# Moving two splits, a maximum and some sums out of the first step of the last stage of a fused kernel

## The chip, the cores and the metric

The kernel runs on one core of a Trainium2 chip. The metric is the device time of one execution, in microseconds (us). Three timed executions of the kernel before gave 990.42, 991.65 and 994.59 us; the median is 991.65 us. All engines (TensorE, here PE, with its weight loads as PEld; VectorE, DVE; ScalarE, ACT; GpSimd, POOL; SyncE, SP, which issues most of the DMAs) run their own instruction lists in program order and wait for one another by semaphores.

## The reference

Three layers in a row, each on the result of the one before:

```python
scores = scale * q @ k.T                       # 4 batches x 8 heads, 576 x 576, head 64
scores = where(scores >= max(scores) - tau, scores, -1e9)
x = softmax(scores) @ v                        # -> 2304 tokens x 512
x2 = ((x @ w1) * (x @ w2)) @ w3 @ w_out        # d_ff 1024
h = x2 @ w_in                                  # d_ff 2048
g = where(h > 0, h, exp(min(h, 0)) - 1)        # ELU
out = g @ w_out2
```

q, k, v and the output are float32, the weights of the last two layers float64.

## The kernel before

The attention and the products x@w1, x@w2 come first; their order is planned by a table, and the change does not touch them. They leave g = (x@w1)(x@w2) in DRAM, and M = w3·w_out in SBUF. What follows is written out by hand: the order of the code is the order on each engine.

**The x stage** makes x2 = g·M. It goes over six blocks of 384 tokens (`TB`), in the order `JS`; a block has four tiles, and tile n = 4·block + e (n = 0 to 23) is 24 matmuls (L1405) into one of four PSUM buffers. Precision is kept by splitting numbers into a high and a low part: g of the next block is loaded by SP into the eight buffers `th`, ACT writes the high parts into `sl` (L326) and DVE the low ones (L327). These eight ACT and eight DVE instructions, called the splits of x→x+1, are issued behind the last tile of each block (n = 3, 7, 11, 15, 19), and the matmuls of the next block read `sl`. ACT copies each finished tile out of PSUM (L1443, L1446), and squares it for a size (L1223, sums in `xm`).

The list `slot[n]` holds other work that is hung behind tile n. For each of four quarters q of w_in (`win_jobs`) it converts two chunks from float64 words to float32 (`conv`: ACT L337, DVE L347, L351, L354), takes their sizes as sums of squares (`size(0)` on ACT, `size(1)` on DVE, L370 and L372, into the columns `wm`), forms four sums s1 to s4 on GpSimd (`both`, L1291), and, for q = 0 and 1, scales and splits the seven parts into `WI` (`directs`: ACT L1313, DVE L1316, the latter called the lows of WI). For q = 2 and 3 the parts are stored in DRAM and split later. The scale needs the size over all partitions: at n = 4, 8, 12 and 16 a matmul with ones on PE (L1227) adds up two columns of `wm`, and DVE reads its result (L1230).

x2's seven sums for the last stage (`BSRC`) are split into `so` / `bs[k]`: high on ACT (`high_b`, L1207), low on DVE (`low_b`, L1211). Three are split in slots, two (k = 3, 4) around the last tile n = 23, and k = 5, 6 in the first step of the last stage.

The chunks of w_out2 (`wo_steps`) are converted, measured and split in `jobs`. A scale for g needs the largest size `wo_two` of any chunk, over all partitions: `everywhere` stores a column of 128 values into DRAM (`mx_dr`, L1006), loads it back as 128 rows of 128 (`mxb`, L1010), and DVE takes the maximum (L1013). Before, a first maximum over four of the eight chunks goes through this at n = 0, 3 and 5, and a second one over all eight at steps 2 and 3 of the last stage.

**The h stage** (the last) has 24 steps s, 8 for each of three pairs of blocks p. A step is seven products (L1555, six matmuls each, two PSUM buffers in turn); product 0 is read by ACT (L1596) and the others by DVE (L1581), which builds four sums `th`; each goes through the ELU (DVE L1481 minimum, ACT L1482 exponential, DVE L1485, ACT L1487 and DVE L1492 for high and low of `gg`). Between the products stand the output matmuls of the step before (L1505, five at a time), none in step 0. GpSimd and ACT split the stored parts of w_in in the same steps (`split_u`: L1388, L1391, L1394, on loads `wr`).

Of the kernel before, what the change touches and what calls it, by code (L numbers as in the profile page):

```python
# [19 lines left out]
P = 128  # L20
# [12 lines left out]
TB = 384  # L33
# [5 lines left out]
ROOM = 2.0 ** -16  # L39
LEAST_X, LEAST = 2.0 ** -45, 2.0 ** -30  # L40
# [229 lines left out]
def attention_moe_moe2(  # L270
# [916 lines left out]
    bs = [slp2.tile([P, 2, 2, TB], F16, name=f"so{i}") for i in range(3)] + [None] * 4  # L1187
# [83 lines left out]
    def win_jobs(q):  # L1271
# [203 lines left out]
    def elu_low(c):  # L1475

        x, name, dst = c["x"], c["name"], c["dst"]

        def one():
            t = c["t"] = tmp("et", f"et{name}", 2)  # L1480
            V.tensor_scalar(t, x, 0.0, None, op0=ALU.min)  # L1481
            A.activation(t, t, AF.Exp)  # L1482

        def two():
            V.scalar_tensor_tensor(x, c["t"], -1.0, x, op0=ALU.add, op1=ALU.max)  # L1485
            h = hop.tile([P, 2, TB], F16, tag="gg", name=f"gg{name}", bufs=8)
            A.activation(h[:, 0, :], x, AF.Copy, scale=c["by"])  # L1487
            dst["h"] = h

        def three():  # L1490
            h = dst["h"]
            V.scalar_tensor_tensor(h[:, 1, :], x, c["by"], h[:, 0, :], op0=ALU.mult, op1=ALU.subtract)  # L1492

        return one, two, three

    def o_mms(p, f, half, dst, first, last):

        j = JS[2 * p + half]
        stop = last or (p == 0 and f == NH // 2 - 1 + (half == 0) * NH)
        again = p == 0 and f % NH >= NH // 2  # L1500
# [41 lines left out]
    for s, (p, f) in enumerate(steps):  # L1542
# [76 lines left out]
        run_jobs(int(s < 3))  # L1619
# [15 lines left out]
        run_jobs(int(s < 3))  # L1635
        if s == 2:
# [4 lines left out]
        if s == 3:  # L1641
# [16 lines left out]
        if s == NH // 2:  # L1658
# [57 lines left out]
```

## Time and profile before

| | |
|---|---|
| timed, three executions | 990.42 / 991.65 / 994.59 us |
| profiled execution | 992.74 us, its span 991.0 us |
| mean granted TensorE clock | 0.988 of full |
| PE busy | 943.4 us, 95% of the span |
| DVE busy | 757.2 us, 76% |
| ACT busy | 572.3 us, 58% |
| POOL busy | 409.2 us, 41% |

A span is the time from the first to the last instruction that the profiler saw; the execution's time is 1.74 us longer. The x stage begins at 509.47 us, the h stage at 621.08 us and ends with the span. In a row of a timeline the first number is the start, the second the time to the end of the group, and the bracket the idle time of the engine before it with what ended it. In a row of a window each engine's busy time stands with its number of instructions, then the granted clock (1.00 is 2.4 GHz, 0.50 is 1.2 GHz), the share of the DMA engines, and GB/s.

### The profile page before, as it was taken

Reading aid. Unit: us, or ns where it says so; the run is one execution under the profiler, and the core shown is the slowest. Engines: PE = TensorE matmul, PEld = TensorE weight load, DVE = VectorE, ACT = ScalarE, POOL = GpSimd, SP = SyncE. Lnnn points to the kernel's source line nnn. Section 1 sums busy time; section 2 is a strip of 40 time slices with the busy share of each in tenths; the row PEclk is TensorE's granted clock in tenths of the full one; section 3 lists DMA queues with packets and bytes.
Section 4 is the critical chain, followed back from the end, with each engine's and each line's share of the span. In section 5 each row is a group of like instructions: output and inputs, shape, how many; then the busy total and the mean of one; then the engine's idle time right before and its main releaser. Section 6 shows DMA issues by size and latency. Waiting matters only on the chain.

```text
span 991.0 us, 17082 instructions
## 1 busy us (share of the span) xinstructions
PE 943.4 (95%) x6086; PEld 692.9 (70%) x6086; DVE 757.2 (76%) x1445; ACT 572.3 (58%) x1003; POOL 409.2 (41%) x553
## 2 busy tenths in 40 slices
PE   7889999989989999999999899699999999999998
PEld 4456788878988988998789899355555555555554
DVE  7889876888777787486668995778878676875664
ACT  5777776888567676255556748654445323542333
POOL 3468775878789897253423312465300000000000
PEclk9999999999999999999999999799999999999999
DMA  8447655565988878775757587232002000010001
GB/s 270 153 131 167 149 166 159 142 177 152 218 166 207 178 170 158 212 260 199 258 147 228 183 270 262 73 107 40 6 1 103 25 1 1 1 64 1 1 1 64
DMA packets 158866, 130.58 MB, mean 132 GB/s; under 512 B 117340, under 2 KB 145468, under 8 KB 154172
## 3 DMA queue, kind: packets, MB, share of 16 engines
q1 hardware_dynamic: 154668, 99.82, 38.0%
q10 hardware_dynamic: 4112, 29.66, 9.2%
q8 instruction: 48, 0.79, 0.3%
q14 instruction: 38, 0.31, 0.1%
HBM read 80.68 MB, written 21.05 MB: 103 GB/s over the span
## 4 chain that ended last, share of the span: by engine, by line
PE 42%; DVE 4%; ACT 3%; issue 1%; DMA 1%; SPq 0%; DVEq 0%; ACTq 0%
PE o L1505 19%; PE h L1555 16%; PE x L1405 6%; DVE sl L327 1%; PE m L1087 1%; DVE w_win L354 0%; ACT WI L1313 0%; DVE WI L1316 0%; DVE w_wo L354 0%; ACT u_win L337 0%; ACT u_win L370 0%; DVE w_w L354 0%; DMA th<-g_dr 0%; DVE th L1581 0%; DVE M L1097 0%
## 5 line engine op out<-in xcount | busy, mean ns | idle before, releaser
L697 PE MATMUL ab<-x,W 128*128 128x256 f32 (+1 forms) x1536 | 223.8, 298 | 5.5 <-DVE g L712 4.4
L697 PEld LDWEIGHTS ab<-x,W 128*128 128x128 f32 x1536 | 207.5, 188 | 14.6 <-issue 6.0
L1505 PE MATMUL o<-WO,gg 128*128 128x512 f16 x864 | 213.8, 380 | 0.0
L1555 PE MATMUL h<-so,WI 128*128 128x384 f16 x1008 | 194.9, 331 | 4.0 <-DVE th L1581 3.4
L1581 DVE SCALAR_TENSOR_TENSOR th<-h,back,th 128x384 f32<-128x384 f32 x168 | 100.8, 613 | 80.8 <-PE h L1555 80.0
L1555 PEld LDWEIGHTS <-WI 128*128 128x128 f16 x1008 | 99.6, 99 | 89.8 <-issue 8.4
L1505 PEld LDWEIGHTS <-gg 128*128 128x128 f16 x864 | 84.9, 98 | 85.6 <-issue 1.3
L537 DVE SCALAR_TENSOR_TENSOR e<-s,st,e 128x576 f32<-128x576 f32 x144 | 115.2, 808 | 24.4 <-ACT e L531 22.0
L548 POOL TENSOR_TENSOR hl<-e,hl 128x512 f16<-128x512 f32 x94 | 110.3, 1173 | 23.7 <-ACT hl L544 20.1
L513 DVE TENSOR_REDUCE st<-s 128x1 f32<-128x576 f32 x144 | 106.0, 749 | 16.0 <-PE s L503 10.0
L1482 ACT ACTIVATE et<-et 128x384 f32<-128x384 f32 x96 | 49.1, 511 | 110.5 <-DVE et L1481 110.5
L1405 PE MATMUL x<-sl,M 128*128 128x384 f32 x576 | 106.8, 345 | 4.8 <-DVE sl L327 3.9
L1405 PEld LDWEIGHTS x<-sl,M 128*128 128x128 f32 x576 | 103.6, 195 | 6.6 <-DVE sl L327 5.5
L531 ACT ACTIVATE e<-s,st 128x576 f32<-128x576 f32 x108 | 78.4, 737 | 25.4 <-POOL st L521 16.5
L1487 ACT ACTIVATE gg<-th,c_late 128x384 f16<-128x384 f32 x80 | 49.2, 615 | 74.0 <-DVE th L1485 73.8
L503 PE MATMUL s<-qk 128*128 128x288 f32 x480 | 82.6, 304 | 4.9 <-DVE e L537 4.0
L544 ACT ACTIVATE hl<-e 128x576 f16<-128x576 f32 x94 | 63.1, 681 | 23.8 <-DMA pt<-hl 14.4
L503 PEld LDWEIGHTS s<-qk 128*128 128x128 f32 x480 | 67.6, 188 | 13.2 <-issue 7.2
L1485 DVE SCALAR_TENSOR_TENSOR th<-et,th 128x384 f32<-128x384 f32 x96 | 54.5, 567 | 6.1 <-ACT et L1482 5.7
L1492 DVE SCALAR_TENSOR_TENSOR gg<-th,c_late,gg 128x384 f16<-128x384 f32 x80 | 49.1, 614 | 0.2 <-ACT gg L1487 0.2
L1087 PE MATMUL m<-WO,w 128*128 128x512 f32 x192 | 44.9, 392 | 2.5 <-DVE M L1097 1.9
L491 PE MATMUL s<-qkp 128*64 128x288 f32 x288 | 40.7, 415 | 6.7 <-ACT pt L589 3.4
(156 smaller groups left out, 1369.9 us busy)
## 6 DMA issues: line engine op xcount, KB each, us to landing
rqk<-in_qk SPq DMA_DIRECT2D x24, 576.0 KB
raw_wo<-in_wo ACTq DMA_DIRECT2D x12, 1024.0 KB
th<-g_dr SPq DMA_DIRECT2D x48, 192.0 KB
raw_w<-in_w SPq DMA_DIRECT2D x8, 1024.0 KB
raw_w<-in_w3t ACTq DMA_DIRECT2D x8, 1024.0 KB
raw_win<-in_win ACTq DMA_DIRECT2D x8, 1024.0 KB
vr<-in_v SPq DMA_DIRECT2D x16, 320.0 KB
g_dr<-g SPq DMA_DIRECT2D x16, 320.0 KB
```

The costliest lines, as they stand in the source:

```text
L503: T.matmul(s[:, n, :HS], q, k[:, c:c + HS], start=(x == 0), stop=(x == len(ops) - 1))
L513: V.tensor_reduce(st[i][:, 0:1], sc[i][:, :, :HS], axis=AX.XY, op=ALU.max if plain else ALU.min, negate=plain)
L531: A.activation(et[i], sc[i][:, :, :HS], AF.Exp, bias=st[i][:, k:k + 1], scale=esc if plain else -1.0)
L537: V.scalar_tensor_tensor(et[i], sc[i][:, :, :HS], st[i][:, 1:2], et[i], op0=ALU.is_ge if p < NPL else ALU.is_le, op1=ALU.mult, accum_out=s ...
L544: A.activation(hl[i][:, :S], et[i].rearrange("p a b -> p (a b)"), AF.Copy)
L548: G.tensor_tensor(t[:, S + 64:], e[:, :512], t[:, :512], op=ALU.subtract)
L697: T.matmul(o[:, :w], wf[:, m, wx, kt, :], x[:, xx, :], start=(kt == 0 and k == 0), stop=(kt == NK - 1 and k == 2),)
L1087: T.matmul(o, w[:, wx, jt * P:(jt + 1) * P], WO1[jt // 2][:, ox, (jt % 2) * 512:(jt % 2) * 512 + 512], start=(k == 0), stop=(k == 23),)
L1405: T.matmul(o[:, :TB], M[:, f, mx, e * P:(e + 1) * P], gh[j, f][:, gx, :], start=(k == 0), stop=(k == 23),)
L1505: T.matmul(po[j, t], dst["h"][:, gx, t * P:(t + 1) * P], WO[f // 2 % 4][:, f // 8, f % 2, wx, :], start=(first and k == 0), stop=(stop and ...
L1555: T.matmul(o[:, :TB], w[:, wx, kt, :], bs[k][:, kt, xx, :], start=(i == 0), stop=(i == 5),)
L1581: V.scalar_tensor_tensor(x, a, bk, b, op0=ALU.mult, op1=ALU.add)
```

## The change

Seven edits, all in the x and h stages; the order of PE's instructions stays as it is. Line numbers of the new kernel are one or two higher here, from the new constant `LATE` on.

1. Five of the `so` buffers are own tiles and two lie in `sl` (three and four before). k = 3 and 4 are split behind n = 20 to 23 in slots, no longer around the last tile.
2. `size(1)` of each quarter moves from beside `conv(1)` to behind the next splits of g (q = 0: from n = 1 to n = 3; q = 1: from 4 to 5; q = 2: from 9 to 11; q = 3: from 13 to 15).
3. GpSimd's four sums of each quarter begin with a copy of one column out of the last `sl`, so they wait for the last split.
4. The first maximum is taken over six chunks, at n = 22, loaded back at n = 23 and read in step 0 behind product 0. The scales of w for pair 0 move from n = 21 to n = 20, and the five small DVE instructions that follow from the maximum (`h_scale`) go behind its reading.
5. With only two late chunks (`LATE` = 6) the rescaling moves from step 4 to 6, the second maximum from step 2 to 4, its reading from 3 to 5, and the last two `h_scale` from step 5 to 7.
6. The jobs of w_out2 run in steps 1 to 3 (0 to 2 before), and `split_u` begins in step 1.
7. In step 0 the ELU's minimum on DVE is replaced by a Relu of −x on ACT.

```diff
-    bs = [slp2.tile(...) for i in range(3)] + [None] * 4
+    bs = [slp2.tile(...) for i in range(5)] + [None] * 2
 ...
         def both():
+            G.tensor_copy(shift, f32(slots[3][:, 1, 1, :1]))
             quarters()
 ...
-        def second():
-            size(0)
-            conv(1)
-            size(1)
-        t0 = ((0, 1, 3), (3, 4, 7), (8, 9, 11), (12, 13, 15))[q]
+        t0 = ((0, 1, 3, 3), (3, 4, 5, 7), (8, 9, 11, 11), (12, 13, 15, 15))[q]
         slot[t0[0]].append(call(conv, 0))
-        slot[t0[1]].append(second)
-        slot[t0[2]].append(both)
+        slot[t0[1]] += [call(size, 0), call(conv, 1)]
+        slot[t0[2]].append(call(size, 1))
+        slot[t0[3]].append(both)
 ...
-    for k, n in enumerate((16, 17, 19)):
+    for k, n in enumerate((16, 17, 19, 20, 22)):
         slot[n].append(call(high_b, k, 0))
-        slot[(17, 19, 20)[k]].insert(0, call(low_b, k, 0))
+        slot[(17, 19, 20, 21, 23)[k]].insert(0, call(low_b, k, 0))
 ...
+    slot[23].append(lambda: behind.pop(0)())
 ...
-            if n == 0:
+            if n == 20:
+                V.tensor_reduce(w_two[:, 4:5], w_two[:, :4], axis=AX.X, op=ALU.max)
+                back_scale((0,))
+            if n == 22:
                 V.tensor_reduce(
-                    shift, cols("wo_two", 8)...[:, :, :2], axis=AX.XY, op=ALU.max
+                    shift, cols("wo_two", 8)...[:, :, :3], axis=AX.XY, op=ALU.max
                 )
                 seen_o = everywhere(shift)
-            if n == 3:
+            if n == 23:
                 seen_o[0]()
-            if n == 5:
-                seen_o[1](o_two[:, 0:1])
-            if n == 21:
-                V.tensor_reduce(w_two[:, 4:5], w_two[:, :4], axis=AX.X, op=ALU.max)
-                back_scale((0,))
-                h_scale((0,), o_two[:, 0:1], c_by)
 ...
-            V.tensor_scalar(t, x, 0.0, None, op0=ALU.min)
-            A.activation(t, t, AF.Exp)
+            if c["first"]:
+                A.activation(t, x, AF.Relu, scale=-1.0)
+                A.activation(t, t, AF.Exp, scale=-1.0)
+            else:
+                V.tensor_scalar(t, x, 0.0, None, op0=ALU.min)
+                A.activation(t, t, AF.Exp)
 ...
-            while ns[0] < min(max(5 * s + k + 1 - (k > 2) - (k > 5), ...
+            while ns[0] < min(max(5 * s - 5 + k + 1 - (k > 2) - (k > 5), ...
 ...
+        if s == 0:
+            seen_o[1](o_two[:, 0:1])
+            h_scale((0,), o_two[:, 0:1], c_by)
 ...
-        run_jobs(int(s < 3))
+        run_jobs(int(0 < s < 4))
 ...
-        if s in (3, 5):
-            h_scale((0,) if s == 3 else (1, 2), o_two[:, 1:2], c_late)
+        if s in (5, 7):
+            h_scale((0,) if s == 5 else (1, 2), o_two[:, 1:2], c_late)
         after(5)
-        if s == NH // 2:
+        if s == LATE:
             rescale(0)
```

On DVE around the splits of x = 2→3 (behind n = 11) the kernel before has, with `w_win_7179` the second chunk of quarter 2, `sl` and `th` the buffers of the splits (the first and the last of eight are shown), and `WI_7168` quarter 1's parts:

```order
L354 SCALAR_TENSOR_TENSOR w_win_7179<-u_win_7177,w_win_7179 128x1024
L372 SCALAR_TENSOR_TENSOR u_win_7177,wm<-w_win_7179 128x1024
L327 TENSOR_TENSOR sl_6377<-th_6381,sl_6377 128x384
...
L327 TENSOR_TENSOR sl_6380<-th_6388,sl_6380 128x384
L1316 SCALAR_TENSOR_TENSOR WI_7168<-s_1_7092,w_to,WI_7168 128x2x256
L1316 SCALAR_TENSOR_TENSOR WI_7168<-w_win_6918,w_to,WI_7168 128x2x256 x2
L1316 SCALAR_TENSOR_TENSOR WI_7168<-w_win_6955,w_to,WI_7168 128x2x256
L1230 TENSOR_REDUCE xg<-x_1_3_7215 128x1
```

and the new kernel, at the same place:

```order
L355 SCALAR_TENSOR_TENSOR w_win_7177<-u_win_7175,w_win_7177 128x1024
L328 TENSOR_TENSOR sl_6377<-th_6381,sl_6377 128x384
...
L328 TENSOR_TENSOR sl_6380<-th_6388,sl_6380 128x384
L1318 SCALAR_TENSOR_TENSOR WI_7166<-s_1_7090,w_to,WI_7166 128x2x256
L1318 SCALAR_TENSOR_TENSOR WI_7166<-w_win_6916,w_to,WI_7166 128x2x256 x2
L1318 SCALAR_TENSOR_TENSOR WI_7166<-w_win_6953,w_to,WI_7166 128x2x256
L373 SCALAR_TENSOR_TENSOR u_win_7175,wm<-w_win_7177 128x1024
L1231 TENSOR_REDUCE xg<-x_1_3_7212 128x1
```

The size that writes a column of `wm` stood ahead of the eight splits and stands behind them and behind four lows of `WI`. PE reads that column with its ones in front of tile 13, in both kernels alike:

```order
L1405 MATMUL x_4_0_7284<-sl_6380,M 128x384 x6
L1227 MATMUL x_4_0_7284<-wm,ones 128x2
L1405 MATMUL x_4_1_7327<-sl_6377,M 128x384 x6
```

On DVE at the start of step 0, the kernel before has the two lows `so` of k = 3 and 4, a piece of a w_out2 conversion, and the first sum of step 0 (L1581, of `h_0_1`):

```order
L1042 RECIPROCAL wo_to<-wo_two 128x1
L1211 SCALAR_TENSOR_TENSOR so_7772<-bq,x_to,so_7772 128x2x384
L1211 SCALAR_TENSOR_TENSOR so_7774<-tq_6728,x_to,so_7774 128x2x384
L347 TENSOR_SCALAR w_wo_7821<-raw_wo_7508 128x1024
L1581 SCALAR_TENSOR_TENSOR th_6382<-h_0_1_7827,back,th_6381 128x384
```

and the new kernel, from the size of the last early chunk to the same sum:

```order
L1043 RECIPROCAL wo_to<-wo_two 128x1
L1429 TENSOR_REDUCE shift<-wo_two 128x1
L1212 SCALAR_TENSOR_TENSOR so_6728<-tq_6730,x_to,so_6728 128x2x384
L1014 TENSOR_REDUCE o_two<-mxb_7741 128x1
L1259 TENSOR_SCALAR out_by<-x_two,w_two 128x1
L1260 TENSOR_SCALAR out_by<-out_by,o_two 128x1
L1261 TENSOR_SCALAR up<-out_by 128x1
L1262 RECIPROCAL up<-up 128x1
L1263 TENSOR_SCALAR c_by<-wo_two,up 128x8
L1575 SCALAR_TENSOR_TENSOR th_6382<-h_0_1_7826,back,th_6381 128x384
```

Between the maximum of a partition (`shift`) and its reading back (`mxb`) there is now one instruction on DVE, and the reading stands ahead of the first sum. SP issues the two transfers around its stores of x2's last tiles:

```order
L1440 DMA x_dr<-x2s_1_7704 128x384
L1007 DMA mx_dr_7739<-shift 128x1
L1440 DMA x_dr<-x2s_2_7742 128x384
L1011 DMA mxb_7741<-mx_dr_7739 128x128
L1440 DMA x_dr<-x2s_3_7775 128x384
L1373 DMA wr_7794<-wi_dr 128x256
```

Before, these two stood a whole block apart among the loads of g, at n = 0 and n = 3.

## Rows read from the trace of the kernel before

**Rows 1.** The page's first part: busy time, share of the span, instructions of each engine.

```profile
PE 943.4 (95%) x6086; PEld 692.9 (70%) x6086; DVE 757.2 (76%) x1445; ACT 572.3 (58%) x1003; POOL 409.2 (41%) x553
```

**Rows 2.** Windows: two stalled blocks, a clean one, steps 0, 1, 3, pair 1's first.

```profile
526.34:546.88 20.54, 19.02 (x99) 18.15 (x98) 16.72 (x26) 12.49 (x29) 6.48 (x5) 0.92 0.64 200
563.80:587.63 23.83, 20.55 (x102) 19.72 (x101) 22.47 (x38) 15.43 (x37) 7.13 (x4) 0.86 0.77 253
587.63:604.35 16.72, 16.72 (x99) 16.72 (x98) 10.56 (x22) 9.11 (x22) 5.42 (x4) 1.00 0.95 321
621.08:640.15 19.07, 10.16 (x45) 4.88 (x45) 15.27 (x24) 10.28 (x21) 9.29 (x12) 0.80 0.29 86
640.15:657.62 17.47, 17.47 (x78) 8.51 (x78) 14.54 (x28) 9.46 (x17) 9.29 (x11) 0.83 0.13 38
672.22:686.81 14.59, 14.59 (x79) 7.63 (x78) 12.14 (x24) 6.12 (x15) 7.93 (x10) 1.00 0.41 57
740.13:759.99 19.86, 19.86 (x107) 10.28 (x105) 18.46 (x35) 11.16 (x20) 0.00 (x0) 1.00 0.00 0
```

**Rows 3.** PE's timeline around tile 12, in the second stalled block.

```profile
568.62 6.36 PE L1405 MATMUL x<-sl,M 128*128 128x384 f32 x20 [0.60 <-DVE sl L327]
574.82 0.28 PE L1227 MATMUL x<-wm,ones 128*128 128x2 f32 x2
```

**Rows 4.** Windows in which PE ran at the lower clock, behind its waits.

```profile
530.00:533.00 3.00, 2.98 (x9) 2.98 (x10) 3.00 (x6) 0.00 (x0) 0.00 (x0) 0.50 0.67 205
568.00:574.00 6.00, 5.40 (x18) 5.38 (x18) 6.00 (x10) 2.42 (x6) 1.97 (x3) 0.50 0.82 241
634.00:645.00 11.00, 8.74 (x26) 3.55 (x25) 6.37 (x20) 7.14 (x14) 2.83 (x4) 0.50 0.09 26
```

**Rows 5.** Windows of eight splits and of three lows of WI, with POOL and without.

```profile
523.64:531.84 8.20, 6.68 (x32) 5.81 (x31) 8.20 (x11) 5.12 (x11) 5.83 (x4) 0.89 0.73 241
550.45:554.59 4.14, 4.14 (x26) 4.14 (x26) 4.14 (x5) 2.06 (x5) 3.37 (x2) 1.00 0.72 244
558.91:560.99 2.08, 2.08 (x14) 2.08 (x13) 2.08 (x4) 2.08 (x4) 0.00 (x0) 1.00 0.91 371
585.91:589.74 3.83, 3.83 (x24) 3.83 (x23) 3.83 (x10) 3.36 (x10) 0.00 (x0) 1.00 0.93 284
```

**Rows 6.** DVE's timeline: the size of quarter 2's second chunk.

```profile
564.25 1.22 DVE L372 SCALAR_TENSOR_TENSOR u_win<-w_win 128x1024 f32<-128x1024 f32 x1
```

**Rows 7.** PE's timeline in step 0.

```profile
633.26 0.61 PE L1227 MATMUL h<-xm,ones 128*128 128x16 f32 x2 [4.91 <-DVE th L1581]
633.71 2.08 PE L1555 MATMUL h<-so,WI 128*128 128x384 f16 x6
```

**Rows 8.** ACT's and DVE's timelines at the end of the x stage.

```profile
620.13 0.92 ACT L1207 ACTIVATE so<-bq,x_to 128x768 f16<-128x768 f32 x1
...
614.95 0.23 DVE L1262 TENSOR_SCALAR c_by<-wo_two,up 128x8 f32<-128x8 f32 x1
615.67 0.16 DVE L1042 RECIPROCAL wo_to<-wo_two 128x1 f32<-128x1 f32 x1
624.75 0.60 DVE L1581 SCALAR_TENSOR_TENSOR th<-h,back,th 128x384 f32<-128x384 f32 x1
```

**Rows 9.** The second maximum's way: SP's waits, SP's and DVE's timelines.

```profile
SPq L1010 <- DMA mx_dr<-o_two: 2.0, 1, 2.0
672.36 0.32 SPq L1006 DMA_DIRECT2D mx_dr<-o_two  x1
680.63 0.32 SPq L1010 DMA_DIRECT2D mxb<-mx_dr  x1
686.61 0.27 DVE L1013 TENSOR_REDUCE o_two<-mxb 128x1 f32<-128x128 f32 x1
```

**Rows 10.** A load from DRAM: SP's issue, POOL's first use of it.

```profile
624.21 32.35 SPq L1374 DMA_DIRECT2D wr<-wi_dr  x16
626.37 2.00 POOL L1388 TENSOR_SCALAR wr<-wr,w_to 128x256 f32<-128x256 f32 x3 [3.93 <-DMA wr<-wi_dr]
```

More of the change, by code (lines that the diff above doesn't have):

```diff
@@ L39 @@
 ROOM = 2.0 ** -16
+LATE = 6
 LEAST_X, LEAST = 2.0 ** -45, 2.0 ** -30
@@ L1186, in attention_moe_moe2 @@
     slp2 = ctx.enter_context(tc.tile_pool(name="slp2", bufs=1, side="right"))
-    bs = [slp2.tile([P, 2, 2, TB], F16, name=f"so{i}") for i in range(3)] + [None] * 4
+    bs = [slp2.tile([P, 2, 2, TB], F16, name=f"so{i}") for i in range(5)] + [None] * 2
     bq = slp2.tile([P, 2, NK, TB], F32, name="bq")
@@ L1205, in high_b @@
         if bs[k] is None:
-            bs[k] = slp.tile([P, 2, 2, TB], F16, tag=f"sl{k - 3}", name=f"so{k}")
+            bs[k] = slp.tile([P, 2, 2, TB], F16, tag=f"sl{k - 5}", name=f"so{k}")
         A.activation(bs[k][:, :, 0, :], BSRC[k], AF.Copy, scale=x_to[:, p:p + 1])
@@ L1334, in directs @@
                 behind.pop(0)()
-        def second():
-            size(0)
-            conv(1)
-            size(1)
-        t0 = ((0, 1, 3), (3, 4, 7), (8, 9, 11), (12, 13, 15))[q]
+        t0 = ((0, 1, 3, 3), (3, 4, 5, 7), (8, 9, 11, 11), (12, 13, 15, 15))[q]
         slot[t0[0]].append(call(conv, 0))
-        slot[t0[1]].append(second)
-        slot[t0[2]].append(both)
+        slot[t0[1]] += [call(size, 0), call(conv, 1)]
+        slot[t0[2]].append(call(size, 1))
+        slot[t0[3]].append(both)
         if q > 1:
-            slot[t0[2] + 2].append(all_out)
+            slot[t0[3] + 2].append(all_out)
         else:
@@ L1414, in attention_moe_moe2 @@
                         load_g(JS[x + 2], f)
-            if x == NB - 1 and e == NK - 1:
-                for k in (3, 4):
-                    high_b(k, 0)
             n = x * NK + e
@@ L1428, in attention_moe_moe2 @@
                 reads.append(lambda q=q, seen=seen: (seen(wg[:, q:q + 1], 1), w_scale(q)))
-            if n == 0:
+            if n == 20:
+                V.tensor_reduce(w_two[:, 4:5], w_two[:, :4], axis=AX.X, op=ALU.max)
+                back_scale((0,))
+            if n == 22:
                 V.tensor_reduce(
-                    shift, cols("wo_two", 8).rearrange("p (a b) -> p a b", a=2)[:, :, :2], axis=AX.XY, op=ALU.max
+                    shift, cols("wo_two", 8).rearrange("p (a b) -> p a b", a=2)[:, :, :3], axis=AX.XY, op=ALU.max
                 )
                 seen_o = everywhere(shift)
-            if n == 3:
+            if n == 23:
                 seen_o[0]()
-            if n == 5:
-                seen_o[1](o_two[:, 0:1])
-            if n == 21:
-                V.tensor_reduce(w_two[:, 4:5], w_two[:, :4], axis=AX.X, op=ALU.max)
-                back_scale((0,))
-                h_scale((0,), o_two[:, 0:1], c_by)
             if x < 2:
@@ L1450, in attention_moe_moe2 @@
             unsized.append((x, e, o[:, :TB]))
-            if x == NB - 1 and e == NK - 1:
-                for k in (3, 4):
-                    low_b(k, 0)
             for fn in slot[n]:
@@ L1498, in o_mms @@
         j = JS[2 * p + half]
-        stop = last or (p == 0 and f == NH // 2 - 1 + (half == 0) * NH)
-        again = p == 0 and f % NH >= NH // 2
+        stop = last or (p == 0 and f == LATE - 1 + (half == 0) * NH)
+        again = p == 0 and f % NH >= LATE
         for t in range(TB // P):
@@ L1563, in after @@
         def after(k, n=5):
-            while ns[0] < min(max(5 * s + k + 1 - (k > 2) - (k > 5), (s - 4) * NC + k + 6), len(USEQ) + 2):
+            while ns[0] < min(max(5 * s - 5 + k + 1 - (k > 2) - (k > 5), (s - 4) * NC + k + 6), len(USEQ) + 2):
                 split_u()
@@ L1586, in quarter @@
             at = 8 * p + f // 2 + (4 if q[0] == "2" else 0)
-            lows[q] = elu_low({"x": x, "name": q + "_" + nm, "dst": gg[q], "by": (c_by if s < NH // 2 else c_late)[:, at:at + 1]})
+            lows[q] = elu_low({"x": x, "name": q + "_" + nm, "dst": gg[q], "first": s == 0,
+                                  "by": (c_by if s < LATE else c_late)[:, at:at + 1]})
             sum_of(x, a, b)
@@ L1611, in attention_moe_moe2 @@
         quarter("11", product(2), m1)
-        run_jobs(int(s < 3))
-        if s == 3:
+        run_jobs(int(0 < s < 4))
+        if s == 5:
             seen_o[0]()
@@ L1618, in attention_moe_moe2 @@
         lows["11"][0]()
-        run_jobs(int(s < 3))
+        run_jobs(int(0 < s < 4))
         after(3)
@@ L1634, in attention_moe_moe2 @@
         lows["11"][2]()
-        run_jobs(int(s < 3))
-        if s == 2:
+        run_jobs(int(0 < s < 4))
+        if s == 4:
             while behind:
@@ L1640, in attention_moe_moe2 @@
             seen_o = everywhere(o_two[:, 1:2])
-        if s == 3:
+        if s == 5:
             seen_o[1](o_two[:, 1:2])
@@ L1657, in attention_moe_moe2 @@
         after(6, 99)
-        if s == NH // 2:
+        if s == LATE:
             rescale(1)
```

## The prediction

> **What bounds the kernel now.** The page's first part comes first: PE is busy for 943.4 of 991.0 us, 95% [rows 1], so only PE's idle or slow time can be won. Then the windows, block by block. A block of the x stage that nothing disturbs takes 16.72 us. The second takes 20.54 (3.8 more) and the fourth 23.83 (7.1 more), both at a mean clock below 1 [rows 2]. In the h stage an undisturbed step takes 14.59 us; step 1 takes 17.47 (2.9 more). Step 0 has only its seven products: a product takes 2.08 us at the lower clock [rows 7], so about 1.04 at the full one and 7.3 for seven; it takes 19.07, 11.8 more [rows 2]. Together 25.6 us stand at the places that the change touches, and they are the most that it can win.
>
> The timelines name the waits. In block 4 PE waits for DVE's low splits [rows 3], and then runs at a granted clock of 0.50, that is 1.2 GHz [rows 4]. In step 0 it waits 4.91 us for DVE's sums [rows 7], and again the clock is 0.50 behind it [rows 4]. DVE is busy for 22.47 of block 4's 23.83 us [rows 2]. So DVE is what PE waits for, and each of its instructions counts there.
>
> **The splits of g (edits 2 and 3).** Eight low splits take 8.20 us when four of GpSimd's sums run beside them, and 3.83 us when none does [rows 5]: (8.20 − 3.83)/4 = 1.1 us for each sum. Tying the sums behind the splits takes this out of the splits, and the size of 1.22 us [rows 6] no longer stands ahead of them. At x = 0→1 they then begin 1.2 us earlier and end 523.64 − 1.2 + 3.8 to 4.9 (paced by ACT's high parts) = 526.3 to 527.3. Block 2 starts at 526.34, and PE reads through the buffers only over its first tile of 16.72/4 = 4.2 us: its stall goes, −3.8 us, and block 3 starts that much earlier. DVE had 16.72 us of work in block 2 [rows 2]; it now fills the shorter block, so at x = 1→2 there is nothing left to win.
>
> But the sums do not go away. Three lows of WI take 4.14 us with two sums beside them and 2.08 alone [rows 5], 1.0 us for each sum: what the splits are spared, the lows pay. This decides at x = 2→3, where the order of DVE is now splits, four lows, size, and PE's ones in front of tile 13 need that size. Before, these splits began when the size was done, at 564.25 + 1.22 = 565.47. Now they begin 1.2 earlier for the size and 3.8 for block 2, but two more of quarter 1's sums now fall on DVE's work ahead of them (+2.2): 562.7. Then 0.4 for ACT's first high part, 3.83 for eight splits: 566.9. Four lows at 2.08/3 = 0.69 make 2.8, the size 1.2, and four sums beside them up to 4 × 1.1 = 4.4, since GpSimd is released at that very moment: 570.9 without, 575.3 with all of them; nearly all fit, so I take 575.1. PE is done with tile 12 about 1 us behind the last split, at 568, and idles for 7 us. It used to pass there at 574.82 [rows 3]. So the two stalls become one: +0.3 us up to here. Behind it PE restarts, and the stretches at 0.50 in rows 4 are at least 3.0 and 6.0 us long; half of that is lost, 1.5 to 3.0, and I take 1.9. The x stage is then 2.2 us longer. The ends: 570.9 with 1.5 gives −2.4, and 575.3 with 3.4 (the lower clock a little longer than the 6.0 shown) gives +4.
>
> The Trainium skill, "SBUF — State Buffer", section "Who interferes with whom", says that a DVE instruction with two inputs in SBUF contends with a GpSimd instruction that reads SBUF. By it the lows and the size, which all have two, would contend as the splits do, so that tying the sums only moves the cost; for the lows the trace agrees (4.14 against 2.08), for the size no run here shows it. Did it not hold here, the x stage would come to the lower end above.
>
> The blocks from x = 3→4 on have DVE busy for 10.56 of 16.72 us [rows 2]; quarter 3's size behind its splits and the two splits of x2 in slots hide there, at nothing. GpSimd's sums of quarter 0 now start at about 527 and take 5.83/4 = 1.5 us each [rows 5], until 533; ACT's parts of WI behind n = 5 wait for them, and its copies of x2 behind those: four PSUM buffers, 16.7 us of PE's work, cover that. The two high parts that ACT gets in the last block are 0.92 each [rows 8], beside a PE that needs nothing of them there.
>
> **Step 0 (edits 1, 4, 6 and 7).** Taken away from DVE: two lows of x2's sums at its start, pieces of the w_out2 jobs and GpSimd's share of the port, four minima (ACT, busy for 10.28 of 19.07 us [rows 2], takes these at nothing). Added: the first sum now stands behind the reading of the maximum. Its way is the long one. DVE finished the last early size at 615.67 + 0.16 = 615.83 [rows 8]; now one more high part of 0.92 stands ahead on ACT, and the reduction follows: SP issues the store at about 617. The only store of this kind that the trace shows with its end was issued at 672.36, and SP, waiting for it, issued the load at 680.63: 8.27 us [rows 9]. So the store lands at 625.2. The load is bounded above by 680.63 to its reading at 686.61, 6.0 us [rows 9], and below by a load from DRAM whose first reader started 626.37 − 624.21 = 2.2 us behind its issue [rows 10]. I take the middle, 4.1: 629.3. With 0.27 for the reading and five small instructions of about 0.23 [rows 8], DVE reads its first product at 630.7, 9.6 us behind the start of the h stage at 621.08; before it did at 624.75, 3.7 behind [rows 8].
>
> From there DVE is much freer, and PE sets the pace. Product 3 needs the PSUM buffer that this sum empties (0.6): four products of 2.08 at the lower clock [rows 7] end at 9.6 + 0.6 + 8.3 = 18.5, where step 0 ended at 19.07. Step 1 was 2.9 us long for the clock; it now comes behind products that follow each other without waits, and I give it half of that back, 1.4. Both steps: −2.0 us. The ends: the load at 2.2 and the clock back at once, −6; the load at 6.0 and step 1 as before, +2.
>
> The Trainium skill, "DMA: Bandwidth & Descriptors", section "Anatomy of one DMA", puts the fixed cost of a DMA at about 2.0 us (measured for GpSimd's own path). By it, store and load together would take about 4 us, as an estimate, and the maximum would be there before it is asked for; the trace disagrees, 8.27 us for the store alone.
>
> **Later steps (edit 5).** The jobs of w_out2 now reach into step 3. Step 1, which has jobs, keeps DVE busy for 14.54 us and step 3 for 12.14 [rows 2]: 2.4 us more, of which the maximum's reading and five scales that leave step 3 give back 1.4. The 13.1 that come out fit into 14.59, though not always beside the right product: +0.5 (0 to 1.5). The ten scales for pairs 1 and 2 stand in step 7 now, 10 × 0.23 at most [rows 8] = 2.3 us right ahead of pair 1's first step, where DVE is busy for 18.46 of 19.86 us [rows 2]: the 0.9 that the 1.4 left can't hold is late, and a little more; +1.0 (0 to 2.3).
>
> **The sum.** +2.2 − 2.0 + 0.5 + 1.0 = +1.7 on the profiled execution's 992.74 us: 994.4. The median of the runs shown is 991.65, 1.1 lower, so 993.4.
>
> **Rivals.** *A, the round trip is hidden.* Place: the first sum of step 0. If store and load land by 624 (7 us together rather than 12.4), PE's long wait goes with its slow clock. Of the 11.8 + 2.9 us at most, the two remaining lows of x2's sums (1 us each) and the restart keep some 4.7: −10 rather than −2. Then −10 + 2.2 + 1.5 = −6.3: 985.4. For it speaks how much work leaves DVE there; against it the 8.27 us. With the x stage at its lower end too it would be 981.
>
> *B, the wait at tile 13 costs its clock.* Place: behind PE's 7 us of idling in block 4. If it stays at the lower clock as long as behind the 4.91 us wait in step 0, where all of 634 to 645 is at 0.50 [rows 4], some 13 us, it loses 6.5 rather than 1.9: x stage +6.8, in all 6.3: 998.0. For it: the wait is longer than any here. Against: that stretch had gaps of its own, and the one at 530 was back at full within a few us. It decides the sign from 10 us of lower clock on.
>
> *How the numbers follow.* A measurement of this kernel can tell about 0.5%, 5 us, from no change: faster is below 986.7, slower above 996.6. My sum has 0.55 (0.44 within, 0.03 below, 0.08 above, its own range 988 to 998), A 0.25 (0.20 below, 0.05 within), B 0.20 (0.17 above, 0.03 within). Faster 0.23, same 0.52, slower 0.25. The range reaches into both: 984 to 1000.
>
> **What would show it.** In the profile after: block 2 within 0.5 us of 16.7; PE's ones in front of tile 13 waiting for DVE's size for 5 to 8 us, with the clock at 0.50 behind; the reading of `mxb` some 9 us into the h stage, PE waiting for the first sum of step 0 for about 6 us, and step 0 at 17 to 20 us. I am wrong if the sums beside the lows cost nothing (no wait at tile 13), or if the store of the maximum lands within 3 us (step 0 under 12 us), or if pair 1's first step is over 22 us.

## The result: 0.7 to 0.8% slower, and the profile after

The changed kernel takes 1000.0 us (median of 6) where the kernel before takes 992.2 (6 runs): a ratio of 1.008, 95% interval 1.0058 to 1.0102. Timed again later it is 1.007 (1.0045 to 1.0096). The forecast was 993.4 us, with no measurable change as the likeliest case; the time lies at the upper end of the range, 984 to 1000, and the loss is more than a measurement's uncertainty. The profiled execution has a span of 997.8 us.

The windows of the changed kernel: the whole x stage (111.61 us before, from 509.47 to 621.08), then steps 0, 1 and 3 and pair 1's first step, which answer to [rows 2]:

```profile
511.09:624.72 113.63, 105.68 (x587) 104.53 (x586) 89.25 (x139) 76.84 (x157) 36.67 (x23) 0.95 0.63 207
624.72:645.18 20.46, 11.89 (x45) 5.40 (x45) 8.48 (x19) 7.74 (x16) 4.30 (x4) 0.68 0.28 64
645.18:661.71 16.53, 16.53 (x79) 8.13 (x79) 12.69 (x27) 7.91 (x15) 3.99 (x6) 0.88 0.08 23
676.30:692.16 15.86, 14.99 (x79) 7.61 (x78) 14.44 (x27) 9.98 (x20) 8.85 (x11) 1.00 0.17 49
750.54:766.79 16.25, 14.92 (x80) 7.62 (x78) 15.14 (x33) 7.60 (x14) 0.00 (x0) 1.00 0.00 0
```

The x stage is 2.0 us longer, step 0 1.4 longer, step 1 0.9 shorter, and two later steps that took 14.6 take 15.9 and 16.3. The row of pair 1's first step in [rows 2], 19.86 us long, begins 5.3 us ahead of that step. By the starts of PE's products the step itself has, in the kernel before:

```profile
745.41:760.01 14.60, 14.60 (x80) 7.64 (x79) 13.27 (x26) 7.60 (x14) 0.00 (x0) 1.00 0.00 0
```

PE's timeline around tile 12, which answers to [rows 3]:

```profile
565.54 0.44 PE L1404 MATMUL x<-sl,M 128*128 128x384 f32 x1 [3.33 <-ACT sl L327]
566.13 5.87 PE L1404 MATMUL x<-sl,M 128*128 128x384 f32 x23 [0.15 <-DVE sl L328]
576.32 0.58 PE L1228 MATMUL x<-wm,ones 128*128 128x2 f32 x2 [4.32 <-DVE u_win L373]
576.76 5.42 PE L1404 MATMUL x<-sl,M 128*128 128x384 f32 x19
```

DVE's timeline in the same place, which answers to [rows 6], and below it the windows of the wait (seven instructions of DVE and five of POOL in it) and of the clock behind it, as in [rows 4]:

```profile
565.52 3.84 DVE L328 TENSOR_TENSOR sl<-th,sl 128x384 fp32r<-128x384 f32 x8 [0.63 <-ACT sl L327]
569.94 4.12 DVE L1318 SCALAR_TENSOR_TENSOR WI<-w_win,w_to,WI 128x512 f16<-128x512 f32 x3
573.98 2.28 DVE L373 SCALAR_TENSOR_TENSOR u_win<-w_win 128x1024 f32<-128x1024 f32 x1
```

```profile
569.42:576.32 6.90, 2.58 (x13) 2.25 (x11) 6.90 (x7) 1.67 (x3) 6.82 (x5) 0.75 0.62 210
577.00:580.00 3.00, 3.00 (x10) 3.00 (x11) 2.55 (x4) 2.05 (x4) 0.38 (x1) 0.50 0.18 66
```

The splits take 3.84 us, undisturbed; the lows behind them take 4.12 rather than 2.08, and the size 2.28 rather than 1.22. PE waits 3.33 us for ACT's first high part ahead of tile 12 and 4.32 us for the size behind it, and restarts at half clock. (By the Trainium skill, "SBUF — State Buffer", section "Who interferes with whom", the size with its two inputs in SBUF contends too; the trace now agrees, 2.28 against 1.22.)

In step 0, SP's timeline answers to [rows 9], DVE's to [rows 8] and PE's to [rows 7]:

```profile
617.42 0.32 SPq L1440 DMA_DIRECT2D x_dr<-x2s  x1
619.58 0.32 SPq L1007 DMA_DIRECT2D mx_dr<-shift  x1
...
627.82 0.32 SPq L1011 DMA_DIRECT2D mxb<-mx_dr  x1
```

```profile
632.01 0.28 DVE L1014 TENSOR_REDUCE o_two<-mxb 128x1 f32<-128x128 f32 x1 [8.40 <-DMA mxb<-mx_dr]
...
633.23 0.61 DVE L1575 SCALAR_TENSOR_TENSOR th<-h,back,th 128x384 f32<-128x384 f32 x1
```

```profile
633.89 4.00 PE L1549 MATMUL h<-so,WI 128*128 128x384 f16 x12 [3.60 <-DVE th L1575]
639.13 0.61 PE L1228 MATMUL h<-xm,ones 128*128 128x16 f32 x2 [1.24 <-DVE th L1575]
639.58 2.08 PE L1549 MATMUL h<-so,WI 128*128 128x384 f16 x6
642.37 2.10 PE L1549 MATMUL h<-so,WI 128*128 128x384 f16 x6 [0.71 <-DVE th L1575]
645.18 2.08 PE L1549 MATMUL h<-so,WI 128*128 128x384 f16 x6 [0.71 <-DVE th L1575]
```

The store of the maximum takes 627.82 − 619.58 = 8.24 us, the load 4.19, and DVE idles 8.40 us. The first sum comes 8.5 us behind the step's start (3.7 before); in two more profiles of the same kernel it came at 9.1 and 10.8, with stores of 8.87 and 9.76 us and loads of 4.03 and 3.48. But behind it PE does not run through: between products it waits 1.24, 0.71 and 0.71 us.

### The profile page after: what moved, and what is told of

It is laid out like the page before. It is cut to its first block, busy times and chain, and to the rows that moved or that the text cites. A ratio compares the mean times of both kernels' runs of the same rounds, so it can differ in the third digit from the quotient of the medians.

```text
span 997.8 us, 17092 instructions
## 1 busy us (share of the span) xinstructions
PE 946.8 (95%) x6086; PEld 695.0 (70%) x6086; DVE 760.2 (76%) x1441; ACT 575.0 (58%) x1007; POOL 412.8 (41%) x557
## 4 chain that ended last, share of the span: by engine, by line
PE 35%; DVE 8%; DMA 3%; ACT 3%; issue 2%; SPq 1%; ACTq 0%; DVEq 0%
PE o L1499 17%; PE h L1549 15%; PE x L1404 2%; DVE sl L328 1%; DVE WI L1318 1%; DMA wi_dr<-w_win 1%; DMA mx_dr<-shift 1%; DVE th L1575 1%; PE m L1088 1%; DVE w_wo L355 1%; DVE w_win L352 1%; DVE w_win L355 0%; DVE u_win L373 0%; DMA x_dr<-x2s 0%; DVE w_win L348 0%
## 5 line engine op out<-in xcount | busy, mean ns | idle before, releaser
L549 POOL TENSOR_TENSOR hl<-e,hl 128x512 f16<-128x512 f32 x94 | 110.2, 1172 | 21.9 <-ACT hl L545 14.5
L1476 ACT ACTIVATE et<-et 128x384 f32<-128x384 f32 x92 | 47.1, 512 | 109.6 <-DVE et L1475 109.6
L1481 ACT ACTIVATE gg<-th,c_late 128x384 f16<-128x384 f32 x72 | 44.3, 615 | 65.9 <-DVE th L1479 65.9
L545 ACT ACTIVATE hl<-e 128x576 f16<-128x576 f32 x94 | 63.3, 680 | 17.5 <-DVE e L538 9.6
L713 DVE TENSOR_TENSOR g<-ab,a 128x256 f32<-128x256 f32 (+1 forms) x64 | 28.9, 452 | 22.9 <-PE ab L698 14.0
```

What stands on the lines that cost most here:

```text
L545: A.activation(hl[i][:, :S], et[i].rearrange("p a b -> p (a b)"), AF.Copy)
L549: G.tensor_tensor(t[:, S + 64:], e[:, :512], t[:, :512], op=ALU.subtract)
```

## The experiments

The first stretch, ahead of the x stage, does the same work in all kernels (four of them load a unit matrix more). The table gives what lies behind it, from the starts of PE's rows in each profile, in us: the x stage, steps 0 and 1 together, step 3, all from step 5 on, and the whole from the start of the x stage; and the time as a ratio to the kernel before.

| kernel | x starts at | x stage | steps 0+1 | step 3 | from 5 | whole | ratio (95%) |
|---|---|---|---|---|---|---|---|
| before | 509.5 | 111.61 | 36.54 | 14.59 | 289.5 | 481.5 | 1 |
| before_1, _2, _3 | 513.3, 514.3, 514.0 | 111.72, 111.63, 111.75 | 36.61, 35.48, 34.45 | 14.6 | 289.5 | 481.7, 480.5, 479.6 | |
| after | 511.1 | 113.63 | 36.99 | 15.86 | 291.0 | 486.7 | 1.0080 (1.0058–1.0102) |
| after_again | 513.0 | 113.16 | 34.49 | 15.85 | 291.0 | 483.7 | 1.0070 (1.0045–1.0096) |
| after_2 | 514.2 | 113.13 | 37.83 | 15.86 | 291.0 | 487.0 | |
| x_only | 514.0 | 113.75 | 36.30 | 14.6 | 289.5 | 483.6 | 1.0027 (1.0011–1.0043) |
| h_only | 514.2 | 110.33 | 34.29 | 15.86 | 291.0 | 480.7 | 1.0020 (1.0002–1.0037) |
| size_first | 510.3 | 111.23 | 37.36 | 15.86 | 291.0 | 484.6 | 1.0021 (1.0002–1.0040) |
| no_tie | 513.9 | 113.99 | 37.19 | 15.85 | 291.0 | 487.2 | 1.0066 (1.0044–1.0088) |
| mx_pe | 511.8 | 114.14 | 30.02 | 15.85 | 291.0 | 480.2 | 0.9987 (0.9967–1.0008) |
| read_early | 510.5 | 113.05 | 35.17 | 16.21 | 291.0 | 484.8 | 1.0025 (1.0009–1.0042) |
| late_fix | 513.9 | 113.16 | 37.39 | 15.52 | 291.0 | 489.7 | 1.0099 (1.0075–1.0123) |
| all_fix | 514.5 | 111.19 | 26.09 | 15.52 | 291.0 | 476.5 | 0.9972 (0.9954–0.9989) |
| best_new | 513.5 | 111.50 | 25.46 | 16.21 | 289.3 | 471.9 | 0.9927 (0.9902–0.9952) |
| best_old | 514.9 | 112.86 | 25.46 | 16.21 | 289.3 | 473.2 | 0.9942 (0.9921–0.9963) |

**Does the stretch ahead belong to the change?** The kernels before_1 to before_3 are the kernel before, after_again and after_2 the changed one, unedited.

> The kernel before, profiled again, for the stretch ahead of the x stage. If that stretch varies and does not belong to the change, the x stage begins somewhere in 509 to 515 us here too, and the x stage takes 111 to 113 us; if it belongs to the change, it begins at 509 to 510 in each of three.

> As before_1, a second profile: the start of the x stage within 509 to 515 us if the stretch varies, near 509.5 if it doesn't; steps 0 and 1 together 34 to 37 us, as the clock comes back sooner or later.

> As before_1, a third profile: the start of the x stage within 509 to 515 us if the stretch varies, near 509.5 if it doesn't.

> The changed kernel as it is, profiled a third time: x stage 113 to 114 us, steps 0 and 1 together 34.5 to 37, step 3 at 15.9 and pair 1's first step at 16.2 as in the two profiles there are; its x stage begins at 511 to 515 us.

> The changed kernel as it is, timed once more beside the others. The stages of its profile added up to 5.2 us more than before from the start of the x stage, 1.6 came from the stretch ahead of it, and 7.8 was timed. If that stretch varies from run to run and has nothing to do with the change, the ratio here is about 1.005 to 1.006; if it belongs to the change, 1.008 again.

The x stage of the kernel before began at 513.3, 514.3 and 514.0 us in three more profiles, so the 509.5 of the first was an early one, and the stretch is not the change's. From the x stage on the means are 480.8 us (four profiles) and 485.8 (three): +5.0. The second timing, 1.007, was above what I expected without that stretch (1.005 to 1.006), but its interval (4.5 to 9.5 us) holds 5.0 us; the first one's (5.8 to 10.1) does not, so that 2 to 3 us of the timed loss stand in no stage of these profiles. Steps 0 and 1 vary by 2 to 3 us in one and the same program. In part the clock comes back sooner or later: at 641 us in after_again, 14.5 us into step 0, and at 649 in the first profile, 24.4 us into it. In part the store of the maximum varies: in after_2, with 9.76 us, step 0 is the longest, 21.4. A window of each of the two clocks:

```profile
641.00:643.00 2.00, 1.38 (x8) 0.73 (x8) 0.99 (x3) 1.39 (x3) 0.00 (x0) 1.00 0.00 0
```

```profile
646.00:649.00 3.00, 3.00 (x9) 1.18 (x8) 1.78 (x7) 2.88 (x6) 0.00 (x0) 0.50 0.02 5
```

**Which half of the change?** h_only undoes edits 2 and 3; x_only puts these alone into the kernel before.

```diff
 x_only, on the kernel before:
+            G.tensor_copy(shift, f32(slots[3][:, 1, 1, :1]))
-        t0 = ((0, 1, 3), (3, 4, 7), (8, 9, 11), (12, 13, 15))[q]
+        t0 = ((0, 1, 3, 3), (3, 4, 5, 7), (8, 9, 11, 11), (12, 13, 15, 15))[q]
 h_only, on the changed kernel: the same lines back
```

> The changed kernel without its edits 2 and 3 (sizes at their old places, GpSimd's sums not tied), so with the edits of the last stage and x2's splits alone. Theory (the two groups of edits add up: x stage +2.0, the rest +3.2 by the profile, both in the timed 7.8): x stage 111 to 112 us, step 0 20 to 21, time 997 to 998. Rival 1 (the tie costs most of what was lost, in a way the profile's stages do not show): 993 or less. Rival 2 (the tie in itself is a gain, hidden by something else in the x stage): 1001 or more.

> The kernel before with edits 2 and 3 alone (sizes behind the next splits of g, GpSimd's sums tied behind the splits). Theory: the x stage is 113 to 114 us rather than 111.6, all else is as before; time 994 to 995. Rival (the tie costs most of the 7.8 us that were measured): 998 or more. The stretch ahead of the x stage, which no edit touches, tells whether its 1.6 us more in the changed kernel's profile belong to the change: if they do, it is there again with these edits or with those of h_only.

x_only came as the theory had it, 0.27% slower. h_only did not: its x stage of 110.33 us and its step 0 of 18.7 lie below what was expected (111 to 112, 20 to 21), and 0.20% is 2 us where the theory had 5 to 6; rival 1 (at most 0.8) did not hold either. The two halves add up to 0.5%, less than the 0.7 to 0.8 of the whole; the intervals allow for the difference, so an interplay of the halves is neither shown nor ruled out. The x stage is 113.75 us with edits 2 and 3 alone, and step 3 and the end are as before; without them step 3 and the end show the same excess as the changed kernel. x_only's timed 2.7 us is more than its 2.0 by the stages, within its interval. Edits 1 and 7 were not run by themselves.

**The x stage: the size behind the lows, or the tie?**

```diff
 size_first:
-        slot[t0[2]].append(call(size, 1))
+        slot[t0[2]].insert(0 if q == 2 else len(slot[t0[2]]), call(size, 1))
 no_tie:
-            G.tensor_copy(shift, f32(slots[3][:, 1, 1, :1]))
```

> The changed kernel with one edit: quarter 2's size on DVE stands between the splits of x = 2->3 and the four lows of WI, not behind the lows. Theory (the x stage lost its gain because the size waited behind lows that GpSimd's tied sums lengthen): PE's wait of 4.32 us in front of tile 13 goes, and half of the slow clock behind it; the x stage falls from 113.6 to 108 us (107.5 to 109.5), and the time from 1000 to about 994.5. Rival (DVE's whole work sets the block, so the wait only moves to the next thing that PE needs of DVE): the x stage stays at 112 to 114 and the time at 999 to 1000.

> The changed kernel without its edit 3: GpSimd's four sums of each quarter start when w_in is converted, no longer behind the last split of g. Theory (a sum costs DVE about 1.1 us wherever it falls beside two-input work): PE's waits for the splits come back at x = 0->1 and 2->3 (together 2 to 5 us), the wait for the size at tile 13 shrinks from 4.3 to under 2; the x stage is 112.5 to 114.5 us, as with the tie. Rival (the tie is what made the x stage longer): 111 or less.

With the size ahead of the lows the wait at tile 13 is gone, and PE's timeline shows what came in its place:

```profile
564.74 7.57 PE L1404 MATMUL x<-sl,M 128*128 128x384 f32 x24 [3.30 <-ACT sl L327]
572.14 0.28 PE L1228 MATMUL x<-wm,ones 128*128 128x2 f32 x2
572.28 12.73 PE L1404 MATMUL x<-sl,M 128*128 128x384 f32 x72
586.08 0.44 PE L1404 MATMUL x<-sl,M 128*128 128x384 f32 x1 [1.07 <-ACT sl L327]
```

PE still waits 3.30 us for ACT's first high part (3.33 in the changed kernel), which comes behind ACT's own conversions; tile 12 takes 7.4 us at the lower clock instead of 4.2, and PE comes to the next splits earlier than ACT (1.07). Block 4 falls by 4.0 us (25.3 in the mean to 21.35), but blocks 5 and 6 grow by 1.9: the stage falls by 2.1 us (113.3 in the mean to 111.2), which is neither the theory's 108 nor the rival's 112 to 114. It is about what it was before the change (111.7 in the mean); the mended order is no gain by itself. The time fell by 0.5 to 0.6%, as the theory had it; the stage's 2.1 us are 0.2%, and where the rest comes from is open. Without the tie the x stage was 114.0 us: the splits took 5.50 us again and PE's waits for them came back, but the wait for the size stayed at 3.55, more than the 2 I expected: the size took 1.21 us instead of 2.28, but the lows behind the splits took 4.10 as with the tie, and the splits 1.7 us more. So what is spared at one place is paid at another, as the theory had it, and the tie itself neither wins nor loses by more than one profile can tell (114.0 against 113.1 to 113.6 with it).

**Step 0: the round trip, or the buffer?**

```diff
 mx_pe:
+    eye_c = rawp[0].tile([P, P], F32, tag="mxb", name="eye_c", bufs=1)
+    SP.dma_start(eye_c, eye)
-                seen_o = everywhere(shift)
+                V.tensor_scalar(eye_c, eye_c, shift, None, op0=ALU.mult)
             if n == 23:
-                seen_o[0]()
+                T.matmul(o[:, TB:TB + P], ones, eye_c, start=True, stop=True)
+    V.tensor_reduce(o_two[:, 0:1], o[:, TB:TB + P], axis=AX.X, op=ALU.max)
-            seen_o[1](o_two[:, 0:1])
 read_early:
+            if s == 0 and k == 4:
+                ph.append(total(o, xm[:, 8:24]))
-            seen = total(ph[0], xm[:, 8:24])
+            ph[1](xg[:, 1:3], 2)
-            seen(xg[:, 1:3], 2)
```

> The changed kernel with the first maximum's way through DRAM (a store of 8.24 us and a load of 4.19 us) replaced: DVE multiplies a unit matrix by the column, PE sums it with ones behind tile 23, DVE takes the maximum from PSUM. Theory (the round trip is what step 0 waits for): the first sum of step 0 comes about 3 us behind the start of the h stage rather than 8.5, step 0 falls from 20.5 to 12 to 14 us and step 1 from 16.5 to about 15.5; the time falls by 7 to 9 us, to 992. Rival (step 0 is paced by the single PSUM buffer that remains while the sums of x2's sizes sit in product 4's, and by the slow clock, and would be as long): steps 0 and 1 together fall by no more than 3 us, the time to 997.5.

> The changed kernel with the sum of x2's sizes moved in step 0: PE's ones write into product 4's PSUM buffer ahead of its matmuls rather than behind DVE's reading of them, and DVE reads the sum in step 0 rather than in step 1, so that the buffer comes free. Theory (behind the first sum, step 0 is paced by one PSUM buffer, PE and DVE taking turns): the waits of 1.24, 0.71 and 0.71 us go, step 0 falls from 20.5 to 17.5 to 18.5, step 1 stays near 16.5, the time falls by 2 to 3 us. Rival (the lower clock and DVE's own work pace it): step 0 stays at 20 to 20.5.

PE's timeline of mx_pe from the maximum's matmul on:

```profile
625.72 0.38 PE L1436 MATMUL x<-eye_c,ones 128*128 128x128 f32 x2
625.94 4.31 PE L1552 MATMUL h<-so,WI 128*128 128x384 f16 x24
630.54 1.14 PE L1552 MATMUL h<-so,WI 128*128 128x384 f16 x6 [0.30 <-DVE th L1578]
633.25 0.51 PE L1230 MATMUL h<-xm,ones 128*128 128x16 f32 x2 [1.56 <-DVE th L1578]
633.59 2.08 PE L1552 MATMUL h<-so,WI 128*128 128x384 f16 x6
636.39 2.10 PE L1552 MATMUL h<-so,WI 128*128 128x384 f16 x6 [0.72 <-DVE th L1578]
639.20 2.08 PE L1552 MATMUL h<-so,WI 128*128 128x384 f16 x6 [0.71 <-DVE th L1578]
```

Four products run without a wait, and steps 0 and 1 fall to 30.0 us from a mean of 36.4: the round trip cost 6.4 us, near the 7 to 9 that its theory had, and the time fell by 0.8 to 0.9%. Step 0 took 13.3 us, as expected, and step 1 16.75, more than the 15.5 expected. Then the other theory's waits stand there alone, 1.56, 0.72 and 0.71. In read_early they are gone (columns as above; the one that is left is 0.30):

```profile
635.08 2.08 PE L1551 MATMUL h<-so,WI 128*128 128x384 f16 x6 [3.03 <-DVE th L1577]
636.95 0.45 PE L1228 MATMUL h<-xm,ones 128*128 128x16 f32 x2
637.24 3.66 PE L1551 MATMUL h<-so,WI 128*128 128x384 f16 x12
641.20 2.11 PE L1551 MATMUL h<-so,WI 128*128 128x384 f16 x12 [0.30 <-DVE xg L1231]
```

Step 0 took 18.6 us there, just over the 17.5 to 18.5 expected, since the store took 10.1 us in this profile and the first sum came only at 10.9. From that first sum to the end of the step it took 7.75 us, against 11.95, 9.85 and 10.6 in the three profiles of the changed kernel. In the one with 9.85 the clock came back at about the same place of the stretch (5.4 us into it, 6.0 in read_early), so 2.1 us are the shared buffer's own; in the others the lower clock adds to it. The time fell by 0.45 to 0.55% (give or take 0.3), twice the 2 to 3 us expected. Both mends together show it again: steps 0 and 1 took 26.1 us in all_fix against 30.0 with the first alone, and the stretch behind the first sum 6.7 against 11.0. The clock did not fall there at all, so the 4 us hold its share too.

**The later steps.**

```diff
 late_fix:
-        run_jobs(int(0 < s < 4))        (four places)
+        run_jobs(int(0 < s < 3))        (five places)
-        if s in (5, 7):
+        if s in (5, 6):
 best_new, best_old, in place of it:
-        if s in (5, 7):
-            h_scale((0,) if s == 5 else (1, 2), o_two[:, 1:2], c_late)
+        if s == 5:
+            h_scale((0,), o_two[:, 1:2], c_late)
+        if s in (6, 10):                (behind product 0)
+            h_scale((1 + s // 10,), o_two[:, 1:2], c_late)
```

> The changed kernel with two of its late moves halved: the ten jobs of w_out2 run in steps 1 and 2 (five calls a step) and not in step 3, and the scales for pairs 1 and 2 stand in step 6 and not in 7. Theory: step 3 falls from 15.86 to 14.6 to 15.0, pair 1's first step from 16.25 to 14.6 to 15.0, steps 1 and 2 stay within 0.5; together -2.5 us. Rival (the excess goes with DVE's work and only moves): step 2 rises to 15 or more, and step 7 or pair 1's first step stay above 15.5.

> The changed kernel with the four mends together: size ahead of the lows, the maximum over PE, the sum of x2's sizes read early, jobs in steps 1 and 2 and scales in step 6. Theory (the costs stand in different stages and add up: -2.4 in the x stage, -7.2 in step 0 from the maximum, -1.5 there from the reading, now at full clock, -2.5 later): from the start of the x stage to the end about 473 us against 486.7 changed and 481.5 before, time 985, 0.9% faster than before. Rival (DVE becomes what step 0 waits for, and the mends of step 0 overlap): 476 or more from the start of the x stage, 0.995 or more of before.

> The changed kernel with three mends that paid (size ahead of the lows, the maximum over PE, the sum of x2's sizes read early), its jobs in steps 1 to 3, and the scales of pair 1 behind product 0 of step 6 and those of pair 2 behind product 0 of step 10, five instructions at a place. Theory (ten small instructions in a row behind a full stretch of DVE are late wherever they stand, five are covered): from the start of step 5 to the end 289.5 us as before, not 291.0; x stage 111.2, steps 0 and 1 together 26.1; from the start of the x stage to the end 472 us, time 0.990 of before. Rival (the late excess is not the scales'): 291 there, and 473.5.

> The same with the sizes and GpSimd's sums at their places of before (edits 2 and 3 undone). If edits 2 and 3 give nothing by themselves even when mended, the x stage is 110 to 111.5 us and the time 0.989 to 0.990 of before, the same as with them; if the mended order is a gain, the x stage here is 112 or more and the time 0.993.

late_fix was a miss, and its rival held. Step 2 rose to 18.04 us with the jobs packed into it, and the ten scales cost the same in step 6 as in 7 (291.0 from step 5 on in both). The DVE row of late_fix's step 2 and the one of the changed kernel's step 3, with the conversion's last part ahead of it, show the same thing:

```profile
678.57 0.15 DVE L997 TENSOR_SCALAR wo_two<-wo_raw 128x1 int32<-128x1 int32 x1 [1.22 <-ACT u_wo L371]
```

```profile
676.97 1.21 DVE L355 SCALAR_TENSOR_TENSOR w_wo<-u_wo,w_wo 128x1024 int32<-128x1024 int32 x1
...
682.55 0.15 DVE L997 TENSOR_SCALAR wo_two<-wo_raw 128x1 int32<-128x1 int32 x1 [1.19 <-ACT u_wo L371]
683.00 0.60 DVE L1575 SCALAR_TENSOR_TENSOR th<-h,back,th 128x384 f32<-128x384 f32 x1
```

A job isn't only its busy time: DVE stands 1.2 us waiting for ACT's square, in front of a sum that PE needs. PE's wait for that sum is 1.2 of the 3.4 us that step 2 lost in late_fix, and about 0.8 of the 1.3 that step 3 lost in the changed kernel; the rest stands behind other work of DVE and ACT, the conversion of 1.21 us among it. In best_new the scales, five in two places, cost nothing: 289.3 us from step 5 on, as before. all_fix missed its 473 us: its 476.5 and 0.9972 are the rival's numbers, but not by the rival's cause, since its steps 0 and 1 fell by more than expected and the excess is late_fix's (18.2 us in step 2, 291.0 from step 5 on). With the jobs put back, best_new came to 471.9 and 0.9927, a slightly smaller gain than the 0.990 expected; it is 0.7% faster than the kernel before (0.5 to 1.0). best_old, with the order of before in the x stage, is at 0.9942: its interval overlaps, and its 112.9 us there answer neither of my two cases. The same order took 110.3 in h_only: there the clock stayed at 1.00 through block 2 (19.1 us), where behind the same two waits of 0.76 us it fell to 0.50 in best_old (20.7 us). So these profiles don't settle what the order is worth by itself.

## Why the prediction was wrong, step by step

- **The splits and the tie: right in sum, not in course.** Predicted +2.2 us for the x stage; +1.6 in the mean of the profiles. Block 2's stall went (16.87 us). PE passed its ones at 576.32, which is 574.7 by the clock of before (its x stage began 1.62 later), 575.1 forecast; but it had not idled for 7 us there: it waited 3.3 us for ACT ahead of tile 12, ran part of that tile at half clock, and then waited 4.3 for the size (3.7 to 4.4 in three profiles, 5 to 8 named as the sign). DVE's chain set the moment all the same. Tiles 13 to 16 took from 576.76 to 595.37, 18.6 us where four clean ones take 16.7, so the lower clock cost 1.9 behind it as forecast, a figure that was chosen between 1.5 and 3.0 and is luck in part. Rival B's long stretch at half clock did not come here.
- **The maximum's way: right.** In the three profiles 8.24, 8.87 and 9.76 us for the store (8.27 forecast), 4.19, 4.03 and 3.48 for the load (4.1); first sum at 9.4 us in the mean (9.6). Rival A fell with the store.
- **What follows the first sum: the step that failed.** "Four products of 2.08 … end at 18.5" and "products that follow each other without waits" gave −2.0; the means are 35.8 us before and 36.4 after, +0.7. The forecast has 8.9 us from the first sum to the end of step 0; it took 10.8 in the mean (9.85 to 11.95). That is 1.9 of the 2.7 us missed, though in two of the profiles part of it ran at full clock; the rest is step 1, which gave back 0.7 instead of 1.4. Product 4's PSUM buffer holds x2's sizes until DVE reads them in step 1, so products 5 and 6 and the next step's first share one buffer and take turns with DVE. The waits (1.24, 0.71, 0.71) make up 2.66 us, and read_early removed them (7.75 us in place of 10.8). The last two were there in the timeline of before, behind the longer wait of 4.91 us that [rows 7] shows, and counted as part of it:

```profile
636.50 2.10 PE L1555 MATMUL h<-so,WI 128*128 128x384 f16 x6 [0.71 <-DVE th L1581]
640.15 2.08 PE L1555 MATMUL h<-so,WI 128*128 128x384 f16 x6 [1.55 <-DVE th L1581]
```

- **Step 3: mis-sized.** Predicted +0.5, measured +1.3: I compared busy times with the length of the step, and DVE's wait for ACT is in neither.
- **The ten scales: mis-sized.** Predicted +1.0, measured +1.5. The row that this was read from is not pair 1's first step: 19.86 us is that step and 5.3 us ahead of it. The step took 14.60 us with 1.33 idle on DVE, by chance nearly the 1.4 that I took. That idle time was not at the scales' place, so it covered little of their 2.1 us. The sign "over 22 us" was set from the same row and is 5.3 us too high.

The sum +1.7 should have been +5.0: 2.7 more from the failed step, 1.3 from the two sizes, 0.6 less from the x stage. The forecast's profile was also 4 us early in a stretch that nobody had touched. The timed loss was 6.8 and 7.8 us; of the difference to 5.0 the record shows no cause.

## What to carry to other kernels

When a wait goes, list every buffer and every reader behind it before giving the freed engine its full pace: the next bound here was one PSUM buffer held by a two-column sum. A reduction over partitions that went through DRAM cost 12.4 to 13.2 us of latency here; a matmul with ones on a scaled unit matrix took 0.38 us of PE here, and the reading of its result 0.29 of DVE. Idle time of a step covered an added instruction only at the place where it stood: ten scales in a row cost 1.5 us, five at a time at two places nothing.

## What the runs showed of the hardware

A store of 512 bytes to DRAM took nearly as long here as one of 192 KB: 8.24 us for the first maximum, 8.27 for the second one before, when no store of x2 was on its way; and SP's store of x2's tile 21, issued at 617.42, released ACT's next copy only at 627.16 (9.7 us later, row below), while a load of 64 KB came in 4.19.

```profile
627.16 0.49 ACT L1439 ACTIVATE x2s<-x 128x384 f32<-128x384 f32 x1 [2.46 <-DMA x_dr<-x2s]
```

The return of the clock differs in one and the same program by 10 us (14.5 and 24.4 us into step 0), and steps 0 and 1, with the store's 8.24 to 9.76 us in them, by 3.3 (34.5 to 37.8).

GpSimd's sums lengthen not only DVE's instructions with two inputs. Tied behind the splits of x = 1→2, two of them fall beside conversions of w_in that read one tensor, and each conversion takes 1.1 us longer. The first row is the kernel before without a sum beside it, the second the changed kernel:

```profile
554.51 0.75 DVE L347 TENSOR_SCALAR w_win<-raw_win 128x1024 uint16<-128x1024 uint16 x1
...
553.01 1.86 DVE L348 TENSOR_SCALAR w_win<-raw_win 128x1024 uint16<-128x1024 uint16 x1
```
